# Keys in chunks of 128 with one chunk shared by two heads, in a fused attention and MLP kernel

## The chip, the cores and the metric

The kernel runs on one core of a Trainium2 chip. The metric is the device time of one execution in microseconds (us), taken from several executions; all times here are of executions in the undisturbed ("fast") state. Lower is better. Besides its times, each kernel left one profiled execution: a page of summaries and a trace of every instruction. The span of a profiled execution is a little off the median time (460.4 us profiled against 461.6 us for the kernel before).

## The reference

Attention over 8 batches of 12 heads, 448 tokens, 64 columns a head, with normalised queries and keys; then an MLP on the joined heads. Everything is float32 on the outside.

```python
def rmsnorm(x, g):
    return x / np.sqrt(np.mean(x * x, axis=-1, keepdims=True) + 1e-06) * g

q_n, k_n = rmsnorm(q, g_q), rmsnorm(k, g_k)              # (8, 12, 448, 64)
attn = softmax(q_n @ k_n.T / 8)                          # (cut: written out in the original)
x = (attn @ v).transpose(0, 2, 1, 3).reshape(3584, 768)
h = x @ w_in                                             # w_in (768, 2048)
g = h * (1.0 / (1.0 + np.exp(-1.702 * h)))
out = g @ w_out                                          # w_out (2048, 768)
```

## The kernel before

Heads are taken two at a time: 6 pairs in a batch, 48 in all. A pair goes through this line of stages. The sync queue loads queries, keys and values. ScalarE squares, VectorE sums, GpSimd finishes the norm and multiplies queries and keys into `row` (bf16). For the first 12 pairs TensorE turns `row` into columns; for the other 36 the sync queue does, with a transposing DMA. TensorE then makes the scores, ScalarE the exponential, TensorE the values, VectorE the division, and the sync queue turns the result into `xT` with another transposing DMA. The MLP matmuls `gp` (448 columns) and `op` (384 columns) of earlier batches are woven between. The output rows are stored by the sync queue too.

```python
SS, NS = 112, 4                    # 448 keys = 4 chunks of 112, for each head
N_ATT, N_KZ, N_V, N_RAW, N_SQ, N_QKN = 3, 3, 4, 7, 2, 3   # raw: loads of 7 pairs ahead

def load(i, which):                # one DMA for queries, one for keys, one for values
    src = (q, k, v)[which][b, h0:h0 + 2].rearrange("h (ss ns) d -> ss h ns d", ns=NS)
    ...
    eng = nc.scalar if i == 0 and which == 1 else nc.sync
    eng.dma_start(out=raw[i][:SS, which], in_=src)

def score(i, kc):                  # two matmuls a tile, four tiles a pair: 8 of 448 columns
    sc = scs[i, kc] = ps_sc.tile([128, 2, 512], FP32, tag="sc", name="sc")
    for hp in range(2):
        nc.tensor.matmul(sc[:SS, hp, :S], lhsT=qk_ring[i % N_KZ][:, NS * (1 + hp) + kc, :],
                         rhs=qk_ring[i % N_KZ][:, :NS, :], start=True, stop=True)

def values(i, hp, qs):             # 4 key chunks x 4 query chunks x 2 heads: 32 of 65 columns
    for kc in range(NS):
        nc.tensor.matmul(os_[i, hp][:, qs, :],
                         lhsT=att_ring[i % N_ATT][:SS, kc, hp, qs * SS:qs * SS + WIN],
                         rhs=vx_ring[i % N_V][:SS, hp, kc, :],
                         start=(kc == 0), stop=(kc == NS - 1))
```

The instruction order is not written by hand. A small list scheduler in the kernel simulates all engines with a duration for each task and writes the instructions in the order that it finds; the order on every engine and queue is then fixed. A task's arguments are the engine, the duration in ns, a priority and what it depends on.

```python
od.add(("L", i, w), "SP", 400, lambda i=i, w=w: load(i, w), i - 7 + (0, 0.1, 1.5)[w],
       deps=..., lat=moved(830.0))
od.add(("T", i), "SP", 400, lambda i=i: turn_dma(i), i - 10.0, deps=..., lat=moved(2400.0))
od.add(("X", i), "SP", 400, lambda i=i: back_dma(i), i - 10, deps=..., lat=moved(800.0))
od.add("gG", "DVE", 350, scale_g, -90, at=5000.0)      # product of the two gain vectors
for c in range(4):                                     # weights, by the GpSimd queue
    od.add(("WI", c), "POOL", 900, ..., at=13000.0 + 6500.0 * c, lat=moved(4100.0))
```

Of the kernel before, what the change touches and what calls it, by code (L numbers as in the profile page):

```python
# [9 lines left out]
FP32 = mybir.dt.float32  # L10
# [114 lines left out]

@with_exitstack
def kernel(
# [15 lines left out]
    assert DM == H * D  # L143
    SS = 112
    NS = S // SS
    NP = H // 2
# [24 lines left out]
    for t, src in ((gq, g_q), (gk, g_k)):  # L171
        col = src.rearrange("(d o) -> d o", o=1)
        for lo in (0, 64):
            nc.gpsimd.dma_start(out=t[lo:lo + 64, :], in_=col)  # L174
# [4 lines left out]
    att_ring = [consts.tile([128, NS, 2, AW], BF16, name=f"att{j}", tag=f"att{j}")  # L179
                for j in range(N_ATT)]  # L180

    qk_ring = [consts.tile([128, 3 * NS, SS], BF16, name=f"qk{j}", tag=f"qk{j}")
               for j in range(N_KZ)]


    row_ring = [consts.tile([128, (3 * NS + 1) * 128], BF16, name=f"row{j}", tag=f"row{j}")
                for j in range(N_QKN)]

    def row_view(j, gi):
        t = row_ring[j % N_QKN]  # L190
        if gi == 0 or j < ON_PE:
            t = t[:, gi * NS * 128:(gi + 1) * NS * 128]
            return t.rearrange("p (n h d) -> p h n d", h=2, d=D)
        both = t[:, NS * 128:].rearrange("p (h r) -> p h r", h=2)[:, :, :NS * 128]
        return both.rearrange("p h (n c) -> p h n c", c=128)[:, :, :, :D]

    vx_ring = [consts.tile([128, 2, NS, D + 1], BF16, name=f"vx{j}", tag=f"vx{j}")
               for j in range(N_V)]
    for t in qk_ring:
        nc.vector.memset(t[64:128, NS:2 * NS, :], 0.0)  # L200
        nc.vector.memset(t[0:64, 2 * NS:, :], 0.0)
    for t in vx_ring:
        nc.gpsimd.memset(t[:, :, :, D:D + 1], 1.0)
    for t in att_ring:
        nc.gpsimd.memset(t[:, :, :, S:AW], 0.0)
# [5 lines left out]
    raw_p = pool("raw", N_RAW)  # L211
    vraw_p = pool("vraw", N_RAW)
# [25 lines left out]
    raw, vraw, rs, obs, xT = {}, {}, {}, {}, {}  # L238
# [5 lines left out]
    def load(i, which):  # L244
        b, h0 = i // NP, 2 * (i % NP)
        src = (q, k, v)[which][b, h0:h0 + 2].rearrange("h (ss ns) d -> ss h ns d", ns=NS)
        if which == 2:
            vraw[i] = vraw_p.tile([128, 2, NS, D], FP32, tag="vraw", name="vraw")
            nc.sync.dma_start(out=vraw[i][:SS], in_=src)
            return  # L250
        if which == 0:
            raw[i] = raw_p.tile([128, 2, 2, NS, D], FP32, tag="raw", name="raw")
        eng = nc.scalar if i == 0 and which == 1 else nc.sync
        eng.dma_start(out=raw[i][:SS, which], in_=src)  # L254

    def square(i, part):
        if part.start in (None, 0):
            sq_of[i] = sq_p.tile([128, 2, 2, NS, D], FP32, tag="sq", name="sq")
        nc.scalar.activation(out=sq_of[i][:SS, part], in_=raw[i][:SS, part], func=ACT.Square)  # L259

    def reduce(i, part):
        g0 = group_of[i][0]
        if g0 not in ssq_of:
            ssq_of[g0] = stat_p.tile([128, 3, 2, 2, NS], FP32, tag="ssq", name="ssq")
        nc.vector.reduce_sum(out=ssq_of[g0][:SS, i - g0, part], in_=sq_of[i][:SS, part],  # L265
                             axis=AX.X)


    def stat_of(grp, name):
        t = stat_p.tile([128, 3, 2, 2, NS], FP32, tag=name, name=name)  # L270
        return t, t[:SS].rearrange("p a b c d -> p (a b c d)")[:, :len(grp) * 4 * NS]
# [3 lines left out]
    def seed(grp):  # L275
        x = ssq_of[grp[0]][:SS].rearrange("p a b c d -> p (a b c d)")[:, :len(grp) * 4 * NS]
        _, t = stat_of(grp, "seed")
# [6 lines left out]
    def rsqrt(grp):  # L284
        eng = nc.vector if grp[0] == 0 else nc.gpsimd
        x, t = seed_of[grp[0]]
        y, yf = stat_of(grp, "rs")
        m = len(grp) * 4 * NS
        eng.tensor_tensor(out=yf.bitcast(I32), in0=magic[:SS, :m], in1=t.bitcast(I32),  # L289
# [7 lines left out]
        for p in grp:  # L297
            rs[p] = (y, p - grp[0])

    def norm(i, gi):  # L300
        y, a = rs[i]
        if gi == 1 and ON_PE <= i < ON_PE + N_QKN:
            c = row_ring[i % N_QKN][:, NS * 128:3 * NS * 128].rearrange("p (n c) -> p n c", c=128)
            nc.gpsimd.memset(c[:, :NS, D:], 0.0)
            nc.gpsimd.memset(c[:, NS:, :D], 0.0)
        nc.gpsimd.tensor_tensor(  # L306
            out=row_view(i, gi)[:SS], in0=raw[i][:SS, gi],
            in1=y[:SS, a, gi].to_broadcast([SS, 2, NS, D]), op=ALU.mult)

    def vcast(i):  # L310
        vx = vx_ring[i % N_V][:SS].rearrange("p h n d -> p (h n) d")
        vr = vraw[i][:SS].rearrange("p h n d -> p (h n) d")
        nc.gpsimd.tensor_tensor(out=vx[:, :, :D], in0=vr,  # L313
                                in1=ones[:SS, :].to_broadcast([SS, 2 * NS, D]), op=ALU.mult)
# [12 lines left out]
    def take_q(i):  # L327
        nc.vector.tensor_copy(out=qk_ring[i % N_KZ][:, :NS, :], in_=tps[i][:, 0])
# [281 lines left out]
```

## Time and profile before

| quantity | before |
|---|---|
| time, median of 3 (range) | 461.67 us (461.55 to 461.86) |
| profiled span | 460.4 us |
| TensorE / ScalarE / GpSimd busy | 95% / 70% / 43% of the span |
| TensorE share of the chain that ended last | 88% |
| squares' wait for key loads, all executions of that instruction together | 9.1 us |
| sync queue's records, 100 to 300 us | 66% of the time, 59% without semaphore instructions |

The busy shares and the chain stand on the page. The squares' wait is a line of the view of waits by releaser.

How to read it: TensorE is the limit when its pieces follow each other without a gap, and then the time is the sum of its issue intervals. The prediction shows the lines for that.

### The profile page before, as it was taken

The numbers are of one execution on the slowest core, as the hardware profiler recorded it, in microseconds if no ns is written. First come the engines' busy times: TensorE is split into PE (matmuls) and PEld (weight loads), VectorE is DVE, ScalarE is ACT, GpSimd is POOL, SyncE is SP. The second block draws the span as 40 slices with busy tenths as digits, with TensorE's granted clock in tenths as the row PEclk, the third lists the DMA queues.
The fourth block names the chain that finished last, engine by engine and source line by source line (L and its number), as shares of the span: only waits on it lengthen the run. The fifth ranks groups of instructions, "written<-read, shape, count | busy, mean of one in ns | idle before, by whom it ended". The sixth has DMA issues, their size and how long they took to land.

```text
span 460.4 us, 9576 instructions
## 1 busy us (share of the span) xinstructions
PE 435.3 (95%) x3728; PEld 271.9 (59%) x3728; DVE 219.0 (48%) x471; ACT 324.1 (70%) x463; POOL 196.5 (43%) x319
## 2 busy tenths in 40 slices
PE   0589999999999999999999999999999999999995
PEld 0356666666666665666666665666666665665563
DVE  3777888765653446515572347622551125403400
ACT  4587997888887778967886779866786677614421
POOL 4888986975272544434452635445343000000000
PEclk9997999999999999999999999999999999999998
DMA  8999999966868866587675885575323650021022
GB/s 204 266 243 255 250 244 231 214 185 158 163 136 155 234 160 152 130 186 166 155 168 119 216 192 131 124 172 144 66 57 74 105 121 16 17 78 36 0 70 69
DMA packets 111277, 67.48 MB, mean 147 GB/s; under 512 B 70272, under 2 KB 107648, under 8 KB 111232
## 3 DMA queue, kind: packets, MB, share of 16 engines
q1 hardware_dynamic: 105616, 60.35, 56.0%
q0 software_dynamic: 5376, 6.29, 7.8%
q8 instruction: 29, 0.48, 0.5%
q10 hardware_dynamic: 240, 0.23, 0.2%
q14 instruction: 16, 0.13, 0.1%
HBM read 45.61 MB, written 11.01 MB: 123 GB/s over the span
## 4 chain that ended last, share of the span: by engine, by line
PE 88%; POOL 3%; DVE 2%; DMA 2%; ACT 2%; issue 1%; SPq 1%; POOLq 0%; DVEq 0%; ACTq 0%
PE op L514 32%; PE gp L491 30%; PE sc L350 15%; PE o L362 10%; DMA gk<-in_g_k_dram 1%; POOL row L306 1%; ACT att L355 1%; PE t_ps L322 1%; DMA raw<-in_k_dram 1%; PE ot_ps L385 1%; DVE ssq L265 1%; DVE qk L332 0%; DVE obs L373 0%; POOL gq L174 0%; SPq L254 0%
## 5 line engine op out<-in xcount | busy, mean ns | idle before, releaser
L355 ACT ACTIVATE att<-sc 112x896 bf16<-112x896 f32 x192 | 173.9, 916 | 39.9 <-PE sc L350 37.9
L514 PE MATMUL op<-w_out_s,g 128*128 128x384 bf16 x896 | 167.5, 325 | 0.0
L491 PE MATMUL gp<-xt,w_in_s 128*128 128x448 bf16 x768 | 162.6, 352 | 0.0
L306 POOL TENSOR_TENSOR row<-raw,rs 112x512 bf16<-112x512 f32 x96 | 98.3, 1043 | 94.2 <-DMA qk<-row 84.6
L350 PE MATMUL sc<-qk 128*112 128x448 bf16 x384 | 109.4, 370 | 3.0 <-ACT att L355 1.4
L514 PEld LDWEIGHTS <-g 128*128 128x128 bf16 x896 | 81.1, 97 | 47.4 <-issue 0.3
L506 DVE SCALAR_TENSOR_TENSOR g<-th,gp 128x448 bf16<-128x448 f32 x128 | 78.0, 615 | 60.9 <-ACT th L500 60.8
L491 PEld LDWEIGHTS <-w_in_s 128*128 128x128 bf16 x768 | 71.0, 98 | 57.8
L362 PEld LDWEIGHTS <-att 112*128 112x128 bf16 x1536 | 82.2, 99 | 36.8 <-DVE obs L373 1.5
L500 ACT ACTIVATE th<-gp 128x448 f32<-128x448 f32 x128 | 69.3, 543 | 35.3 <-PE gp L491 35.1
L362 PE MATMUL o<-vx,att 112*128 112x65 bf16 x1536 | 90.8, 196 | 0.7 <-ACT att L355 0.4
L313 POOL TENSOR_TENSOR vx<-vraw,ones 112x512 bf16<-112x512 f32 x48 | 50.0, 1042 | 51.6 <-PE o L362 35.8
L265 DVE TENSOR_REDUCE ssq<-sq 112x16 f32<-112x1024 f32 (+1 forms) x50 | 58.4, 1174 | 27.9 <-ACT sq L259 27.7
L372 DVE RECIPROCAL rcp<-o 112x4 f32<-112x4 f32 x96 | 17.4, 181 | 112.0 <-PE o L362 111.4
L259 ACT ACTIVATE sq<-raw 112x1024 f32<-112x1024 f32 (+1 forms) x50 | 50.9, 1022 | 14.3 <-DMA raw<-in_k_dram 9.1
L524 ACT ACTIVATE osb<-op 128x384 f32<-128x384 f32 x56 | 27.3, 487 | 40.4 <-PE op L514 40.4
L350 PEld LDWEIGHTS <-qk 128*112 128x112 bf16 x384 | 44.0, 135 | 17.9 <-issue 4.0
L373 DVE TENSOR_TENSOR obs<-o,rcp 112x256 bf16<-112x256 f32 x96 | 40.7, 424 | 3.3
L343 ACT ACTIVATE qk<-qk,gG 128x448 bf16<-128x448 bf16 x36 | 23.9, 663 | 1.0 <-DMA qk<-row 0.9
L322 PE MATMUL t_ps<-ident,row 112*128 112x112 bf16 x96 | 9.6, 250 | 15.8 <-POOL row L306 15.7
L322 PEld LDWEIGHTS <-row 112*128 112x128 bf16 x96 | 7.2, 117 | 19.0 <-POOL row L306 17.5
L289 POOL TENSOR_TENSOR rs<-magic,seed 112x48 int32<-112x48 int32 (+1 forms) x16 | 4.5, 282 | 20.0 <-DVE seed L280 16.9
(37 smaller groups left out, 90.1 us busy)
## 6 DMA issues: line engine op xcount, KB each, us to landing
raw<-in_q_dram SPq DMA_DIRECT2D x48, 224.0 KB, 4.2
vraw<-in_v_dram SPq DMA_DIRECT2D x48, 224.0 KB, 3.9
raw<-in_k_dram SPq DMA_DIRECT2D x47, 224.0 KB, 4.7
w_in_s<-in_moe_w_in_dram POOLq DMA_DIRECT2D x4, 768.0 KB, 12.8
w_out_s<-in_moe_w_out_dram POOLq DMA_DIRECT2D x4, 768.0 KB, 11.3
out_dram<-osb SPq DMA_DIRECT2D x8, 336.0 KB, 3.3
out_dram<-osb SPq DMA_DIRECT2D x8, 288.0 KB, 2.7
out_dram<-osb SPq DMA_DIRECT2D x8, 240.0 KB, 2.9
```

The lines of the kernel that those rows point to most:

```text
L259: nc.scalar.activation(out=sq_of[i][:SS, part], in_=raw[i][:SS, part], func=ACT.Square)
L265: nc.vector.reduce_sum(out=ssq_of[g0][:SS, i - g0, part], in_=sq_of[i][:SS, part], axis=AX.X)
L306: nc.gpsimd.tensor_tensor(out=row_view(i, gi)[:SS], in0=raw[i][:SS, gi], in1=y[:SS, a, gi].to_broadcast([SS, 2, NS, D]), op=ALU.mult)
L313: nc.gpsimd.tensor_tensor(out=vx[:, :, :D], in0=vr, in1=ones[:SS, :].to_broadcast([SS, 2 * NS, D]), op=ALU.mult)
L350: nc.tensor.matmul(sc[:SS, hp, :S], lhsT=qk_ring[i % N_KZ][:, NS * (1 + hp) + kc, :], rhs=qk_ring[i % N_KZ][:, :NS, :], start=True, stop=True)
L355: nc.scalar.activation(out=att_ring[i % N_ATT][:SS, kc, :, :S], in_=scs.pop((i, kc))[:SS, :, :S], func=ACT.Exp)
L362: nc.tensor.matmul(os_[i, hp][:, qs, :], lhsT=att_ring[i % N_ATT][:SS, kc, hp, qs * SS:qs * SS + WIN], rhs=vx_ring[i % N_V][:SS, hp, kc, : ...
L373: nc.vector.tensor_tensor(out=obs[i][:SS, :, hp, :], in0=o[:SS, :, :D], in1=rcp[:SS, :].to_broadcast([SS, NS, D]), op=ALU.mult)
L491: nc.tensor.matmul(ps[:, :], lhsT=w_in_s[:, ki, m * 128:(m + 1) * 128], rhs=xT[b][:, ki, :], start=(ki == 0), stop=(ki == KI - 1))
L500: nc.scalar.activation(out=th[:, :], in_=gps[b, m][:, :], func=ACT.Tanh, scale=0.851)
L506: nc.vector.scalar_tensor_tensor(out=g_of[b // 2][:, m, lo:lo + S], in0=ths.pop((b, m))[:, :], scalar=1.0, in1=gps.pop((b, m))[:, :], op0= ...
L514: nc.tensor.matmul(ops[bp, tm, hf][:, :], lhsT=g_of[bp][:, ko, tm * 128:(tm + 1) * 128], rhs=w_out_s[:, ko, hf * HALF:(hf + 1) * HALF], st ...
```

## The change

448 is 3 x 128 + 64. From the third batch on, a head's keys are three chunks of 128 and a tail of 64, and the tails of both heads share one chunk. That is 7 score matmuls a pair where there were 8, and all of them use the whole width of the array. The values follow: one matmul of 130 columns serves both heads' tails, with zeros in the other head's place. The loads of keys and values become three DMAs: one for the 2 x 384 rows, and one for each head's tail, which has to land on its own half of the partitions. GpSimd's multiplies are cut along the same line. Partition rows that the narrow form leaves unwritten must be zero, hence seven memsets at the start, and the gain vectors move from GpSimd's queue to the sync queue.

```diff
+    NB = 3
+    NC = 2 * NB + 1
+    TAIL = NB * 128
...
-    for t, src in ((gq, g_q), (gk, g_k)):
-        col = src.rearrange("(d o) -> d o", o=1)
-        for lo in (0, 64):
-            nc.gpsimd.dma_start(out=t[lo:lo + 64, :], in_=col)
...
+    for t in raw_ring:
+        nc.gpsimd.memset(t[96:128, :QW], 0.0)
...
     def load(i, which):
...
+        if which == 0 or not wide(i):          # as before: one DMA
...
             return
+        nc.sync.dma_start(out=by_head(t, (NB + 1) * D, NB * D, lo),
+                          in_=src[:, :TAIL].rearrange("h (p j) d -> p h (j d)", j=NB))
+        for h in range(2):
+            nc.sync.dma_start(out=t[HALVES[h], lo + NB * D:lo + (NB + 1) * D],
+                              in_=src[h, TAIL:])
...
+        for c in chunks(i, t):                 # 7 chunks in 4 tiles
+            nc.tensor.matmul(sc[parts_of(i), c % 2, :S], lhsT=keys, rhs=queries(i),
+                             start=True, stop=True)
...
+        one(NB, o, vx[:, NB:NB + 2, :], start=True, stop=False)   # 130 columns
+        for h in range(2):
+            for j in range(NB):
+                one(c, o[:, h, :], vx[:, c + h, :], ...)          # 65 columns
...
-    od.add("gG", "DVE", 350, scale_g, -90, at=5000.0)
+    od.add("Lg", "SP", 1700, load_g, PLACE["G"], lat=3000.0)
+    od.add("gG", "DVE", 350, scale_g, PLACE["gG"], deps=["Lg"])
...
-            od.add(("L", i, w), "ACTQ" if i == 0 and w == 1 else "SP", 400,
+            od.add(("L", i, w), "ACTQ" if i == 0 and w == 1 else "SP",
+                   1200 if w_ and w else 400,
```

(Cut: the same tiles as rings with views for both widths, the divisions' new layout, durations of the order's model.)

## The prediction

> **What bounds the kernel now.** I read the page first (busy shares, the 40 slices, the chain that ended last), then the chain in order of time for a steady stretch, then the groups by shape, then the timeline of the first 20 us.
>
> ```profile
> PE 435.3 (95%) x3728; PEld 271.9 (59%) x3728; DVE 219.0 (48%) x471; ACT 324.1 (70%) x463; POOL 196.5 (43%) x319
> PE   0589999999999999999999999999999999999995
> PE 88%; POOL 3%; DVE 2%; DMA 2%; ACT 2%; issue 1%; SPq 1%; POOLq 0%; DVEq 0%; ACTq 0%
> ```
>
> TensorE is busy in every slice but the first few and the last, and 88% of the chain that ended last is TensorE following itself. Busy time alone is no proof (ends of matmuls are modelled), so I looked at how closely the pieces follow each other:
>
> ```profile
> 204.52 0.13 PE o L362 x4
> 204.65 0.40 PE sc L350 x2
> 205.05 1.30 PE op L514 x8
> ...
> 209.22 0.38 PE sc L350 x2
> 209.60 0.65 PE op L514 x4
> 210.25 0.26 PE o L362 x8
> ```
>
> Each piece starts where the last one ends; nobody is waited for. So from about 55 us to the end the time is the sum of TensorE's issue intervals, and any interval that goes comes off the end. From start to start in the records between 100 and 400 us, the means are: 189 ns a score or gp matmul (448 columns), 162.5 an op (384), 32.2 a value matmul (65 columns). One oddity: a score pair takes 0.38 us after an MLP matmul but 0.40 after a value matmul. In the records the first score after a value matmul takes 209 ns and not 189 (68 of 68 cases, of 284 scores in that stretch).
>
> ```profile
> L350 PEld LDWEIGHTS <-qk 128*112 128x112 bf16 x384 | 44.0, 135 | 17.9 <-issue 4.0
> L362 PEld LDWEIGHTS <-att 112*128 112x128 bf16 x1536 | 82.2, 99 | 36.8 <-DVE obs L373 1.5
> ```
>
> The weight load of a score, 112 columns wide, takes 135 ns; all loads of 128 columns take 97 to 99. Behind a 32 ns value matmul the longer load is not hidden.
>
> The start is another regime. TensorE's first matmul is at 13.7 us:
>
> ```profile
> 0.75 0.90 SPq L254 DMA_DIRECT2D raw<-in_q_dram  x2
> 9.62 0.56 DVE L397 TENSOR_TENSOR gG<-gq,gk 128x1 f32<-128x1 f32 x1 [3.00 <-DMA gk<-in_g_k_dram]
> 12.61 2.04 POOL L306 TENSOR_TENSOR row<-raw,rs 112x512 bf16<-112x512 f32 x2 [2.46 <-DVE rs L296]
> ```
>
> VectorE stands 3.00 us for the gain vectors, fetched by GpSimd's queue, though only the key scaling needs them; behind that wait stand the eleven small operations of the first pair's norms (10.28 to 12.53 us), and behind these the first norm multiply at 12.61.
>
> **What the Trainium skill says.** (1) "TensorE: Matmul & The Clock Gate", section "Back-to-back issue gap", gives N/2.4 + 2.5 ns warm: 189.2 for 448 columns, 162.5 for 384. The trace agrees to the tenth. For 65 columns it gives 29.6 where I measure 32.2, so something else adds 2.6 ns there. For the new 130-column matmul I use 56.7. (2) The same page, section "Weight-path perf modes — Fast Weight Load (FWL) and DoubleRow", says the fast load needs exactly 128 weight columns. The 135 against 99 ns above agrees. (3) "DMA: Bandwidth & Descriptors", section "Why small descriptors are slow (HBM only)": a fixed cost for each packet. In the trace's packet records the median is 18 ns for 256 bytes, 46 for 1024 and 121 for 3072, that is 9 ns plus 0.0365 a byte: the fixed part is there and small. (4) "GPSIMD Engine Reference", section "Reconciling with measured numbers": a dispatch cost for each instruction and some 2.6 cycles an element; the trace's 1043 ns for 512 columns against 286 for 48 gives 208 ns fixed plus 1.63 ns a column.
>
> **The change part by part.** The first 12 pairs (two batches) keep their form; 36 pairs change.
>
> Scores, on the path: 7 in place of 8 a pair. 36 x 189 ns = **6.8 us off**.
>
> Values, on the path: 32 matmuls of 65 columns become 24 of 65 and 4 of 130 (one holds both heads' 64 tail keys, other head's values zero). 32 x 32.2 = 1030 ns; 24 x 32.2 + 4 x 56.7 = 1000 ns. 36 x 0.03 = **1.1 us off**.
>
> Weight loads, on the path: the key chunks are now 128 columns wide, so the 209 ns should become about 192 (what gp takes after a value matmul in the records). 68 cases among 284 scores, thus about 69 in 288: 69 x 17 ns = **1.2 us off**.
>
> Sum for TensorE: 9.1 us. The built program has 3548 matmuls in place of 3728, with the same 768 gp and 896 op.
>
> The start, on the path: the gain vectors now come by the sync queue and VectorE's order has them after the first norms, so the 3.0 us wait is off the chain. Against it stand seven new memsets of 32 x 512 on GpSimd before all else, and in the built program each query load waits for its memset. I estimate 0.52 us for one: the trace's memsets took 204 ns for 128 columns and 310 for 256, so 0.83 ns a column. The first query load then issues near 2.0 instead of 0.75 us. It lands near 5.0 and not 4.6 because the queue is shorter behind the key load. Then sum of squares near 6.9, norm chain to 9.2, first norm multiply at 9.3 instead of 12.6. Further on the gain shrinks: the second pair's key load is later in the queue, VectorE waits for it, and the first scores I put at 14.2 instead of 16.6. Before the first MLP matmul the scalar engine's order has one more square (1.06 us) than before, with equal counts of exponentials. Net **1.7 us off** (2.4 less some of the 1.06).
>
> Beside the path: ScalarE evacuates a single chunk in the fourth score tile, 543 ns (the row of the tanh, same 448 columns) for 916: 36 x 0.37 = 13 us less. VectorE reduces 960 columns for 1024: about 2 us less. GpSimd pays: the key multiply and the value copy become four instructions each, 2 x (208 + 192 x 1.63) + 2 x (208 + 64 x 1.63) = 1.67 us for 1.04. That is 36 x 1.25 = 45 us more, some 245 us in all (54%), still far from a bound. DMA: a key or value load is 256 packets of 768 bytes plus 128 of 256 in place of 224 of 1024: 11.8 for 10.3 engine-us, little. It is three issues instead of one on the sync queue, 36 x 4 x 0.42 = 60 us more issue time, on a queue that loads pairs seven ahead.
>
> I add **0.6 us** for waits that do not exist now: 461.7 - 9.1 - 1.7 + 0.6 = **451.5**, rounded to 451.3 since the start may give its whole 2.4.
>
> **The rivals.** (a) The start gives nothing or loses: the memsets of GpSimd may run slower than 0.83 ns a column (f32 and not bf16), and the loads of pairs 0 to 2 queue behind four tiny transfers. For it speaks that everything before 20 us hangs on the loads; against it that the 3 us wait is plainly removed. Then 453 to 454. (b) The scalar engine becomes the wait: squares of later pairs already wait for key loads (9.1 us in ten cases in the waits by releaser, the longest 2.6), and these loads now land about 1 us later, being three issues; a scalar stall past some 2 us would hold the PSUM tiles and so TensorE. Against it: the scheduler's order in the built program was made with the longer loads, and ScalarE has 13 us more room. At its worst 36 x 0.1 = 4 us: 455. (c) The score's extra 20 ns is not the narrow load; then 1.2 us less gain: 452.5. (d) GpSimd falls behind between 60 and 100 us, where it is 74 to 80% busy in the windows and the first wide pairs, with their extra memsets, begin; the values would wait for their copies. Its later waits for the row transposes (84.6 us) say there is room: at most 2 us. (e) Upward: the start gives 4 us: 449.
>
> **Range and chances.** The TensorE sum is firm, 8 to 9.5 us: 452.2 to 453.7 by itself, all but at the 2% line of 452.4. The start decides the side. With my 1.7 it is faster; with (a) or (b) within 2%. Predicted 451.3, 449.0 to 454.3, faster 0.67, within 2% 0.32, slower 0.01 (no engine comes near a new bound).
>
> **What the profile after would show.** Right: TensorE still in nearly all of the chain; 252 wide scores at 189 ns, also behind value matmuls, with loads near 99 ns; the 130-column ones about 57 ns apart; first matmul between 10 and 12 us; first scores near 14. Wrong: idle time before score or op matmuls put down to ScalarE, VectorE's first reduce later than 5.3 us by over 2, squares waiting much more than 9 us in total for key loads, or the value matmuls of 65 columns no longer 32 ns.

## The result and the profile after

| | before | after |
|---|---|---|
| time, median (range), 4 runs each, same chip | 461.61 us (461.06 to 461.86) | 467.00 us (465.40 to 467.55) |
| ratio after / before (95% interval) | | 1.0113 (1.0084 to 1.0141) |
| profiled span | 460.4 us | 465.5 us |

The kernel became 1.1% slower, which is still within 2%. A ratio here is always the mean time of one kernel's fast runs over the mean of the other's of the same rounds, so it is not quite the ratio of the medians in the table. The prediction was 451.3 us with a range from 449.0 to 454.3; the result is well outside.

First the page of the changed kernel: busy time of each engine, the 40 slices of TensorE, and the chain that ended last, by engine and by line.

```profile
PE 427.3 (92%) x3548; PEld 259.0 (56%) x3548; DVE 215.3 (46%) x471; ACT 306.1 (66%) x463; POOL 233.7 (50%) x543
PE   0767899999999988999899998999999999999995
PE 66%; DMA 17%; issue 5%; SPq 4%; POOL 3%; ACT 2%; DVE 2%; ACTq 0%; POOLq 0%; DVEq 0%
```

TensorE has 180 matmuls less and is busy 8 us less, as hoped, but its slices now show 8s in the middle. The chain holds 66% TensorE where it held 88%. What came in its place is DMA with 17%, and the sync queue (SPq) with 4%.

How much time TensorE stood still is read from the view of windows. Its columns are the window, its length, then busy us (and instructions) of PE, PEld, DVE, ACT and POOL, then the granted clock (the share of TensorE's full clock that it was given), the DMA engines' share and GB/s. Before, then after:

```profile
140.00:180.00 40.00, 39.82 (x356) 25.24 (x355) 17.15 (x38) 31.05 (x45) 16.98 (x24) 1.00 0.77 171
180.00:220.00 40.00, 40.00 (x352) 25.35 (x350) 17.31 (x36) 31.00 (x45) 19.18 (x33) 1.00 0.73 167
```

```profile
140.00:180.00 40.00, 36.85 (x312) 22.47 (x311) 12.82 (x29) 24.51 (x39) 23.94 (x61) 1.00 0.77 172
180.00:220.00 40.00, 37.97 (x316) 22.88 (x314) 18.63 (x40) 31.39 (x48) 23.18 (x59) 1.00 0.66 158
```

TensorE stood for 3.15 and 2.03 us in these two windows, and hardly at all before. Over the whole stretch from 60 to 400 us the same view gives 339.46 us busy of 340 before and 329.98 after: 0.5 against **10.0 us idle**. In these two windows the granted clock is 1.00 on both sides, and the DMA engines' share is not higher than before.

What it waited for is read from the view of waits by releaser. Its columns are the total us, the number of times and the longest wait. Before, then after:

```profile
ACT sq L259 <- DMA raw<-in_k_dram: 9.1, 10, 2.6
ACT qk L343 <- DMA qk<-row: 0.9, 1, 0.9
```

```profile
ACT sq L300 <- DMA raw<-in_k_dram: 26.2, 19, 2.9
ACT qk L416 <- DMA qk<-row: 8.0, 7, 2.4
```

ScalarE's squares wait 26 us for key loads where they waited 9, and its scaling of the turned queries waits 8 us for the transposing DMA where it waited 1. ScalarE itself has less to do than before, but it stands in order, so these waits hold the exponentials behind them.

The next view is the chain in order of time (start us, us, what) around one of the stalls of the changed kernel. "SPq" is the sync queue issuing.

```profile
172.31 0.42 SPq L652
...
173.17 0.41 SPq L291
...
174.83 0.58 SPq L291
...
175.46 0.48 SPq L294
175.94 0.04 issue
175.98 4.13 DMA raw<-in_k_dram
...
180.22 1.01 ACT sq L300
...
182.53 0.42 DVE obs L469
182.95 0.54 DVE g L623
...
183.53 1.29 PE gp L608 x6
```

The key load, 4.13 us from the end of its issue to its landing, is the last link before the square. It is in the queue behind an output store (L652) and a value load (L291 and L294), and the chain goes through all of them: the queue worked them off one after another. After the square, VectorE's sum, division and gate follow, and the gate (g) is what the MLP matmul at 183.53 waits for.

The timeline of the sync queue shows the same stretch from its own side: start us, us, line, operation, tile, and xN where N DMAs are folded into one row. Before, then after:

```profile
171.47 1.90 SPq L338 DMA_TRANSPOSE qk<-row  x1
173.81 1.20 SPq L392 DMA_TRANSPOSE xt<-obs  x1
175.12 0.52 SPq L249 DMA_DIRECT2D vraw<-in_v_dram  x1
178.51 0.31 SPq L254 DMA_DIRECT2D raw<-in_q_dram  x1
```

```profile
169.95 1.69 SPq L412 DMA_TRANSPOSE qk<-row  x1
171.76 0.97 SPq L652 DMA_DIRECT2D out_dram<-osb  x2
173.17 0.41 SPq L291 DMA_DIRECT2D vraw<-in_v_dram  x1
173.64 1.14 SPq L294 DMA_DIRECT2D vraw<-in_v_dram  x2
174.83 0.58 SPq L291 DMA_DIRECT2D raw<-in_k_dram  x1
175.46 1.13 SPq L294 DMA_DIRECT2D raw<-in_k_dram  x2
176.68 1.23 SPq L490 DMA_TRANSPOSE xt<-obs  x1
```

Before, the queue has pauses: nearly 3 us between 175.64 and 178.51. After, one issue follows the other with hardly a gap. Counted over 100 to 300 us the queue's records fill 66% of the time before and **89%** after. Part of that is semaphore instructions, which issue nothing; the DMA issues alone fill 59% before and **87%** after. With the mean lengths of its records in that stretch this can be added up for one pair, in us:

| for one pair | before | after |
|---|---|---|
| transposing DMA of queries and keys | 1.57 | 1.59 |
| transposing DMA of the result | 1.30 | 1.30 |
| query load | 0.46 | 0.61 |
| key load | 0.53 | 0.50 + 2 x 0.51 |
| value load | 0.68 | 0.71 + 2 x 0.57 |
| output stores | 0.44 | 0.56 |
| sum | 4.98 | 7.43 |

24 pairs pass in these 200 us, so a pair has 8.3 us. 4.98 of 8.3 is 0.60 and 7.43 of 8.3 is 0.89; the direct counts are 0.59 and 0.87, since not quite every DMA of 24 pairs falls into the stretch. The semaphore instructions are the rest: 0.07 before, most of it ahead of the transposing DMAs, and 0.02 after.

What the change was made for did come. The groups by shape, in the changed kernel (busy us and mean ns after the bar):

```profile
L430 PEld LDWEIGHTS <-qk 128*128 128x128 bf16 x252 | 22.9, 98 | 15.8
L454 PE MATMUL o<-vx,att 128*128 128x130 bf16 x144 | 31.8, 221 | 3.4 <-DVE obs L469 3.4
```

The wide score's weight load takes 98 ns where the narrow one took 135, and there are 252 of them, 7 for each of the 36 pairs. From start to start, a score behind a value matmul now takes 188.6 ns and not 209. The 130-column matmul takes 57 to 58 ns from start to start.

### The profile page after: what moved, and what is told of

Same layout as the page of the kernel before. It is cut to its first block, busy times and chain, and to the rows that moved or that the text cites. A ratio compares the mean times of both kernels' runs of the same rounds, so it can differ in the third digit from the quotient of the medians.

```text
span 465.5 us, 9795 instructions
## 1 busy us (share of the span) xinstructions
PE 427.3 (92%) x3548; PEld 259.0 (56%) x3548; DVE 215.3 (46%) x471; ACT 306.1 (66%) x463; POOL 233.7 (50%) x543
## 4 chain that ended last, share of the span: by engine, by line
PE 66%; DMA 17%; issue 5%; SPq 4%; POOL 3%; ACT 2%; DVE 2%; ACTq 0%; POOLq 0%; DVEq 0%
PE op L631 26%; PE gp L608 24%; DMA raw<-in_k_dram 9%; PE sc L430 9%; DMA vraw<-in_v_dram 8%; PE o L454 6%; POOL row L349 2%; SPq L288 1%; ACT sq L300 1%; SPq L294 1%; PE o L446 1%; DVE g L623 1%; POOL vx L349 1%; SPq L291 1%; ACT att L435 1%
## 5 line engine op out<-in xcount | busy, mean ns | idle before, releaser
L435 ACT ACTIVATE att<-sc 128x896 bf16<-128x896 f32 (+1 forms) x192 | 159.7, 846 | 32.0 <-PE sc L430 31.3
L349 POOL TENSOR_TENSOR row<-raw,rs 64x64 bf16<-64x64 f32 (+3 forms) x204 | 115.4, 588 | 83.1 <-DMA qk<-row 55.4
L430 PE MATMUL sc<-qk 128*128 128x448 bf16 (+1 forms) x348 | 100.5, 366 | 6.3 <-ACT att L435 4.2
L313 DVE TENSOR_REDUCE ssq<-sq 128x15 f32<-128x960 f32 (+2 forms) x50 | 56.2, 1127 | 60.4 <-ACT sq L300 56.8
L349 POOL TENSOR_TENSOR vx<-vraw,ones 128x192 bf16<-128x192 f32 (+2 forms) x156 | 66.7, 446 | 29.6 <-PE o L454 13.3
L300 ACT ACTIVATE sq<-raw 128x960 f32<-128x960 f32 (+2 forms) x50 | 48.9, 983 | 34.4 <-DMA raw<-in_k_dram 26.2
L454 PEld LDWEIGHTS <-att 128*128 128x128 bf16 x1008 | 53.0, 98 | 28.4 <-DVE obs L469 4.7
L454 PE MATMUL o<-vx,att 128*128 128x65 bf16 (+1 forms) x1008 | 57.8, 198 | 5.4 <-DVE obs L469 3.4
L641 ACT ACTIVATE osb<-op 128x384 f32<-128x384 f32 x56 | 27.3, 487 | 40.5 <-PE op L631 40.4
L446 PEld LDWEIGHTS <-att 112*128 112x128 bf16 x384 | 18.9, 103 | 9.0 <-ACT att L435 1.9
L446 PE MATMUL o<-vx,att 112*128 112x65 bf16 x384 | 21.4, 201 | 1.8 <-ACT att L435 1.3
L397 PE MATMUL t_ps<-ident,row 112*128 112x112 bf16 x96 | 9.8, 255 | 13.9 <-POOL row L349 13.7
```

What stands on the lines that cost most here:

```text
L300: nc.scalar.activation(out=sq_of[i][parts_of(i), part], in_=raw_ring[i % N_RAW][parts_of(i), part], func=ACT.Square)
L313: nc.vector.reduce_sum(out=stats(i, ssq_of[g0])[:, part.start // D:part.stop // D], in_=sq_of[i][parts_of(i), part].rearrange("p (c d) -> ...
L349: nc.gpsimd.tensor_tensor(out=out, in0=in0, in1=by, op=ALU.mult)
L430: nc.tensor.matmul(sc[parts_of(i), c % 2, :S], lhsT=keys, rhs=queries(i), start=True, stop=True)
L435: nc.scalar.activation(out=att_of(i)[parts_of(i), c.start:c.stop, :S], in_=scs.pop((i, t))[parts_of(i), :len(c), :S], func=ACT.Exp)
L446: nc.tensor.matmul(o[:, w, :], lhsT=att[:SS, 2 * kc + u, w * SS:w * SS + WIN], rhs=vx[:SS, u * NS + kc, :], start=(kc == 0), stop=(kc == N ...
```

## The experiments

Fourteen kernels ran. All gave correct results. A kernel is compared with runs of the kernel before on the same chip. The table gathers what is used below: median time, ratio to the kernel before with its 95% interval, TensorE's idle time between 60 and 400 us (340 less the busy time in the view of windows), and the share of the time between 100 and 300 us that the sync queue's records fill, first all records, then DMA issues alone. (The expectations speak of the first of these.) The last three are from the profiled execution.

| kernel | us | ratio (95%) | idle us | sync records / issues |
|---|---|---|---|---|
| before | 461.6 | 1 | 0.5 | 0.66 / 0.59 |
| after | 467.0 | 1.0113 (1.0084 to 1.0141) | 10.0 | 0.89 / 0.87 |
| 1 before, loads in three | 466.17 | 1.0099 (1.0072 to 1.0127) | 4.2 | 0.85 / 0.81 |
| 2 before, small packets | 465.54 | 1.0082 (1.0064 to 1.0100) | 2.0 | 0.68 / 0.62 |
| 3 before, start of after | 465.32 | 1.0076 (1.0054 to 1.0099) | 0.7 | 0.64 / 0.58 |
| 4 after, one tail DMA | 455.47 | 0.9860 (0.9833 to 0.9887) | 1.0 | 0.74 / 0.73 |
| 5 after, start of before | 464.55 | 1.0075 (1.0047 to 1.0104) | 7.6 | 0.90 / 0.89 |
| 6 before, gain product late | 463.66 | 1.0041 (0.9992 to 1.0091) | 0.0 | 0.63 / 0.58 |
| 7 = 4 + 5 | 455.77 | 0.9854 (0.9807 to 0.9901) | 0.9 | 0.74 / 0.72 |
| 8 = 4, memsets late | 456.17 | 0.9879 (0.9841 to 0.9917) | 0.8 | 0.72 / 0.71 |
| 9 = 4, weights late | 460.75 | 0.9959 (0.9901 to 1.0016) | 6.9 | 0.73 / 0.71 |
| 10 = 7, weights late | 452.93 | 0.9810 (0.9781 to 0.9840) | 0.3 | 0.74 / 0.72 |
| 11 before, weights late | 468.22 | 1.0145 (1.0123 to 1.0166) | 2.9 | 0.61 / 0.58 |
| 12 = 6, weights late | 464.19 | 1.0053 (1.0023 to 1.0083) | 1.2 | 0.63 / 0.58 |
| 13 after, stores elsewhere | 462.18 | 1.0004 (0.9982 to 1.0027) | 6.2 | 0.85 / 0.84 |
| 14 = 10, stores elsewhere | 457.22 | 0.9878 (0.9838 to 0.9918) | 4.8 | 0.70 / 0.68 |

The theory after the first comparison was that the middle of the kernel is lost to the sync queue's issue time, and that the start loses by its own. The rivals were the smaller packets of the tails (256 bytes), GpSimd's longer copies, and the start alone.

How single a change is can be read from the traces, by comparing the order of the instructions on each engine with that of the kernel which was edited. In experiments 1, 2 and 4 every engine runs the same instructions in the same order, but for the number of load issues on the sync queue; in 8 (compared with 4) only the seven memsets stand elsewhere. In all the others the scheduler found another order on every engine: in 3 and 6, for instance, some 740 of TensorE's 3728 matmuls stand elsewhere. Those runs show what a version costs, but not cleanly what the one edit costs.

### 1. The kernel before with its loads cut in three

Nothing else of the change is in this kernel: same widths, same packets.

```diff
+    def send(eng, t, src, i):
+        cuts = (0, SS) if i < ON_PE else (0, 48, 80, SS)
+        for lo, hi in zip(cuts, cuts[1:]):
+            eng.dma_start(out=t[lo:hi], in_=src[lo:hi])
...
-            nc.sync.dma_start(out=vraw[i][:SS], in_=src)
+            send(nc.sync, vraw[i], src, i)
...
-        eng.dma_start(out=raw[i][:SS, which], in_=src)
+        send(eng, raw[i][:, which], src, i if which else 0)
```

> The kernel before, but from pair 12 on each key and value load is cut into three DMAs by partitions (48, 32, 32); packets stay 1024 bytes, no other instruction moves on any engine. Theory A (the sync queue's issue time is the new limit): its share between 100 and 300 us rises from 0.65 to about 0.9 as in the changed kernel, squares wait over 20 us for key loads instead of 9, and the time rises by 5 to 10 us, to 467-471. Rival B (smaller packets or the transposes of 128 rows delay the loads) and rival C (GpSimd's longer norms and copies): nothing of theirs is in this kernel, so 461.7 within 1 us.

It took 466.17 us, 4.5 us more than the kernel before. The queue's share rose to 0.85, the squares' wait for key loads to 17.6 us in 16 cases, and TensorE idled 4.2 us. Each of these is just under what was expected. So more issues alone do cost time here; they do not make the whole 10 us at this share.

### 2. The kernel before with small packets

```diff
+        src = (q, k, v)[which][b, h0:h0 + 2]
+        src = src.rearrange("h (ns ss) d -> ss h ns d", ns=NS) if which and i >= ON_PE else \
+            src.rearrange("h (ss ns) d -> ss h ns d", ns=NS)
```

One DMA a load as before, but every key and value packet is 256 bytes and not 1024, which is worse than in the changed kernel.

> The kernel before, but from pair 12 on keys and values are fetched in runs of 256 bytes (896 packets a load instead of 224), still one DMA for a load; keys are permuted alike in both, so the result stays right. Theory A (issue time): a load is still one issue, so the time stays within 1.5 us of 461.7 unless the issue itself takes longer with more packets (then by as much as the queue's share shows). Rival B (DMA packets): this more than doubles the packet time of a load (16 engine-us for 10), over what the change added, so the loss must be at least that of the change in mid-kernel, 8 to 10 us.

It took 465.54 us, 3.9 us more than the kernel before: over the 1.5 us that theory A allowed, and under the 8 that rival B asked for. Where, the view of windows shows:

```profile
60.00:100.00 40.00, 38.08 (x336) 23.91 (x335) 29.58 (x59) 31.06 (x43) 28.35 (x53) 0.96 1.10 216
100.00:140.00 40.00, 40.00 (x356) 25.02 (x355) 22.94 (x48) 33.99 (x50) 23.07 (x42) 1.00 0.73 157
```

There is a stall of 1.9 us before 100 us, soon after the first small-packet loads, and next to nothing after it, at a queue share of 0.68. The clock of 0.96 there is, by the trace's clock records, a stretch of 3.4 us, from 82.3 us, at half the clock, in which a matmul of 448 columns took 373 ns and not 189; that is worth some 1.7 us (an estimate, half of the stretch). So small packets came with a loss before 100 us, but they do not make the stalls of the middle. The same run shows that the issue time goes with the number of DMAs far more than with their packets: a key load of four times as many packets took 0.53 us to issue, as before, and a value load 0.75 for 0.68.

### 3. The kernel before with the start of the changed kernel

The seven memsets, the gains by the sync queue and the late product, without any wide chunk.

```diff
-            nc.gpsimd.dma_start(out=t[lo:lo + 64, :], in_=col)
+    for t in raw_ring:
+        nc.gpsimd.memset(t[96:128, 0], 0.0)
...
-    od.add("gG", "DVE", 350, scale_g, -90, at=5000.0)
+    od.add("Lg", "SP", 1700, load_g, -5.2, lat=3000.0)
+    od.add("gG", "DVE", 350, scale_g, -0.5, deps=["Lg"])
```

> The kernel before with only the start of the changed one: seven memsets of the raw tiles ahead of all else on GpSimd, the gain vectors by the sync queue after the first four loads, VectorE's product of them after the first norms. Theory D (the start costs): first score near 15.0 us as in the changed kernel, but loads of pairs 7 to 9 land 4 to 6 us later than before, squares wait for them, and TensorE has 3 to 4 us less work done by 60 us: time 464.5 to 466. Rival E (the start is harmless, TensorE's deficit at 60 us in the changed kernel comes from the wide loads that begin at 42 us): 459.5 to 461.7.

It took 465.32 us. The start of the changed kernel, with the order that the scheduler then finds, costs 3.7 us; the prediction had it as a gain of 1.7. Hardly any of it is idle time after 60 us, so it is lost before that.

### 4. The changed kernel with two DMAs a load

The tails of two neighbouring heads can be read in one DMA if the heads are cut the other way: the first head gives its first 384 keys to the wide chunks and its last 64 to the shared chunk, the second head its last 384 and its first 64. The two tails then lie next to each other in memory as 128 rows. The order of keys does not matter to attention. Everything else stays: widths, GpSimd's copies, the start.

```diff
         nc.sync.dma_start(out=by_head(t, (NB + 1) * D, NB * D, lo),
-                          in_=src[:, :TAIL].rearrange("h (p j) d -> p h (j d)", j=NB))
-        for h in range(2):
-            nc.sync.dma_start(out=t[HALVES[h], lo + NB * D:lo + (NB + 1) * D],
-                              in_=src[h, TAIL:])
+                          in_=bass.AP(tensor=src.tensor, offset=src.offset,
+                                      ap=[[NB * D, 128], [(TAIL + 128) * D, 2], [1, NB * D]]))
+        nc.sync.dma_start(out=t[:, lo + NB * D:lo + (NB + 1) * D],
+                          in_=src.rearrange("h s d -> (h s) d")[TAIL:TAIL + 128])
```

> The changed kernel with two DMAs instead of three for each wide key and value load: both heads' tails are taken as the 128 rows that lie together in memory (the last 64 of one head, the first 64 of the next), same bytes and packets, no other instruction moves. Theory A: two issues of some 0.55 us less a pair of about 9 us, the sync queue's share falls from 0.90 to about 0.78, squares wait some 12 us instead of 26, and the time falls by 4 to 7 us, to 460-463. Rivals B and C: packets and GpSimd work are the same, so 466 to 467.

It took **455.47 us**: 11.5 us less than the changed kernel and 1.4% faster than the kernel before. Theory A had expected 4 to 7 us, so it had the direction and not the size. Its windows:

```profile
140.00:180.00 40.00, 40.00 (x337) 24.28 (x334) 18.02 (x38) 31.15 (x50) 24.98 (x64) 1.00 0.86 182
180.00:220.00 40.00, 39.68 (x333) 24.01 (x332) 18.61 (x40) 29.02 (x45) 21.11 (x55) 1.00 0.75 173
```

```profile
ACT sq L300 <- DMA raw<-in_k_dram: 12.0, 9, 2.5
```

TensorE is full again, and the squares' wait is back near its old 9.1 us. Tail packets are as small and GpSimd's copies as long as in the changed kernel, and every engine runs the same instructions in the same order but for the one issue less in each load, so neither is the cause.

### 13. The changed kernel with its stores on another queue

Experiment 4 changes the loads themselves, so it could be that three transfers are late in themselves and the queue has no part in it. This one leaves every load as it is and takes other work off the queue.

```diff
-            nc.sync.dma_start(
+            nc.scalar.dma_start(
                 out=out[b * S:(b + 1) * S].rearrange(...)
...
-            od.add(("D", bp, tm), "SP", 1200, ...
+            od.add(("D", bp, tm), "ACT", 1000, ...
```

> The changed kernel with nothing different but the queue of its output stores: they are issued by the scalar engine's queue, which evacuates the rows that they store. No load, packet, tile or matmul differs. Theory Q (issue time on the sync queue): some 60 stores of 0.48 us, 29 us, leave the sync queue, so its busy share between 100 and 300 us falls from 0.90 to about 0.83; by the two points on hand (0.85 share cost 4.5 us in the first experiment, 0.76 next to nothing) the stall of 10 us between 140 and 320 us should shrink to 3 to 5, the squares' wait for key loads from 26 to about 17, and the time fall by 4 to 7 us, to 460 to 463; the scalar engine has 27 us more to do and may give 1 us back. Rival T (a load in three transfers is late in itself, whatever else the queue does, since three completions must come in): the stall stays, 466 to 468. Rival G (the GpSimd engine's longer copies hold the chain): the same, 466 to 468.

It took 462.18 us, 4.8 us less than the changed kernel, inside what the queue theory gave and outside what the two rivals gave. The share fell to 0.85, a little less than expected, and the squares' wait to 19.8 us. The idle time between 140 and 320 us fell from 9.5 to 5.2 us, where 3 to 5 had been expected. That is not far from experiment 1, which came to nearly the same share from the other side, by adding issues to the kernel before. But the scheduler gave every engine another order here, so this run alone does not isolate the queue.

Rival T can be settled in the traces. From the start of its first issue to its last landing, a key load between 100 and 300 us took 3.46 us (median) in three DMAs in the changed kernel, 3.68 in two in experiment 4, and 3.89 in one in the kernel before. Three transfers are not late in themselves; they are issued late. With experiments 1 and 4, in which only the number of issues differs, this shows the cause in the middle: it is the issue time on this queue.

### 5 to 8. The start

Experiment 5 takes the start of the change back in the changed kernel: gains by GpSimd's queue, memsets by VectorE just before the first wide pairs use the tiles.

```diff
-    for t in raw_ring:
-        nc.gpsimd.memset(t[96:128, :QW], 0.0)
+        if which == 0 and ON_PE <= i < ON_PE + N_RAW:
+            nc.vector.memset(t[96:128, :QW], 0.0)
...
-    od.add("Lg", "SP", 1700, load_g, PLACE["G"], lat=3000.0)
-    od.add("gG", "DVE", 350, scale_g, PLACE["gG"], deps=["Lg"])
+    od.add("gG", "DVE", 350, scale_g, PLACE["gG"], at=9500.0)
```

> The changed kernel, still three issues a wide load, but with the start of before: gain vectors by GpSimd's queue at once, no memsets ahead of the loads (each raw tile's bottom rows are cleared by VectorE just before its first wide use); VectorE's product of the gains stays behind the first norms. Theory D (the start of the changed kernel costs 3 to 4 us): 462.5 to 464.5, with the mid-kernel losses of 10 us still there. Rival E (its start deficit comes from the wide loads at 42 us or from scatter): 466 to 468.

It took 464.55 us, 2.4 us less than the changed kernel's median (467.00, of another chip's rounds); the two intervals overlap, so a gain is not sure. In its trace 25.3 us of matmul work had begun by 60 us (24.1 in the changed kernel, counted with the steady issue intervals), and the idle time after 60 us is 2.4 us less, so at most a part of the difference lies in the start.

Experiment 6 makes the one edit in the kernel before that the prediction counted on: VectorE multiplies the gains after the first norms. (The scheduler's order changes with it.)

```diff
-    od.add("gG", "DVE", 350, scale_g, -90, at=5000.0)
+    od.add("gG", "DVE", 350, scale_g, -0.5, at=9500.0)
```

> The kernel before with one move: VectorE's product of the gains behind the first pairs' norms, so the 3.0 us wait is gone; loads as before. The prediction's step (that wait is on the path, worth about 2 us at the end): 459.3 to 460.3, first score near 14.3 us. Rival F (the start is limited by the loads, which land 0.86 us apart, and by the weight loads that share the DMA engines, so an earlier first score is given back): 461 to 463, with the same lost TensorE time by 60 us, 32 us.

The first scores came at 14.0 us and not 16.6, as the prediction says, and yet the time was 463.66 us, with an interval that holds "no change" and leaves out a gain of more than 0.1%. A wait was taken away on the chain to the first score, and the end did not come earlier. The first MLP matmul started at 57.9 us, where the kernel before has it at 55.0. A rival that no run separates is TensorE's clock: before 60 us it stood at half for 13.7 us in this trace and for 6.8 us in the kernel before, and the fastest of the four runs (459.82 us) had a mean clock of 0.993, the other three (463.47 to 465.79 us) 0.983 to 0.987.

Experiments 7 (4 and 5 together) and 8 (4 with late memsets, but the gains by the sync queue) ask whether start and middle add up.

> One tail issue (as in the fourth run) and the start of before with the late gain product. If mid-kernel issue time and the start are the two causes and add: 455.5 less about 3, 451.5 to 453.5; with lost TensorE time (span less the sum of issue intervals) 38 to 40 us as in the kernel before. If the start's cost was already only scatter in the fourth run (33.1 us lost by 60 us, 32.1 before): 454.5 to 455.5.

> The fourth run's kernel with the memsets taken from ahead of the loads, the gain vectors still by the sync queue: splits the start's cost. If the four gain transfers on the sync queue (2.6 us of issue before the third pair's loads) are the cost: 455 to 456. If the memsets (the first query load at 1.94 instead of 0.75 us) are: 453 to 454, near the run with both mended.

They took 455.77 and 456.17 us, no better than experiment 4. With two DMAs a load, taking the start back is worth nothing that these runs can see. Experiment 8 is the cleanest of these, since nothing but the memsets moved: its first score came at 13.7 us, where experiment 4 has it at 15.7, and the time did not fall. Here too the clock stood at half for longer before 60 us, 17.1 us against 6.8.

### 9 to 12. The weights later

The four loads of `w_in` run beside the key loads of pairs 7 to 9. In the changed kernel these key loads land at 30.8, 36.6 and 40.5 us, and at 25.1, 30.5 and 35.5 before. The theory was that an earlier weight load takes their bandwidth. Each experiment issues `w_in` later in the order's model: 9 in kernel 4, 10 in kernel 7, 11 in the kernel before, 12 in kernel 6.

```diff
-    WI=13000.0, WIs=6500.0, WO=42000.0, WOs=7000.0)
+    WI=19000.0, WIs=6500.0, WO=42000.0, WOs=7000.0)
```

> The fourth run's kernel (one tail issue, start as changed) with the four issues of the first weight matrix some 5 us later in GpSimd's order; they landed at 30 to 49 us and the first MLP matmul comes at 56. Theory W (an earlier start only lets the weights share the DMA engines before the loads of pairs 7 to 9 are in, so their squares wait): those key loads land by 26, 30 and 35 us instead of 31, 37 and 41, TensorE has lost 31 to 32 us by 60 us instead of 33 to 36, and the time falls from 455.5 to 451.5-453.5. If the weights don't matter: 455 to 456.

> The seventh run's kernel (one tail issue, start of before, gain product late) with the weights some 5 us later: theory W 450 to 452.5, because the first score is 1 to 2 us sooner than in the kernel before and is kept; if the weights don't matter: 455 to 456.

> The kernel before with the weights some 5 us later alone, as control. Before, the loads of pairs 7 and 8 already landed 3 to 5 us ahead of their squares, only pair 9 waited 1.14 us, so theory W gives little: 459.5 to 461.5. If it gains over 3 us, the weights' place was a fault of the kernel before and not something the change brought about.

> The sixth run's kernel (the kernel before, gain product late, first score at 14.0 us instead of 16.6, yet 463.7 us) with the weights some 5 us later. Theory W: the early start is now kept, 458.5 to 460, TensorE's lost time by 60 us 29 to 31 us instead of 34.7. If the cause is another (slower loads from the start on, or TensorE's clock falling to half): 462.5 to 464.

The key loads came earlier in all four (pair 9 at 28 to 33 us), as foreseen. The times did not follow. Experiment 10 is the best kernel with **452.93 us**, 1.9% faster than the kernel before. Experiment 9 lost 5 us against kernel 4, experiment 11 lost 6.5 us against the kernel before, and experiment 12 changed nothing (464.19 against 463.66), which its expectation had kept for another cause. In experiment 9 the loss has moved:

```profile
60.00:100.00 40.00, 33.69 (x284) 21.04 (x282) 25.82 (x55) 26.84 (x39) 25.76 (x57) 0.91 0.86 196
```

TensorE stands for 6.3 us there, and the clock of 0.91 is two stretches of 3.4 us at half (from 65.2 and 78.8 us), worth another 3.4 us (an estimate, half of both). Two squares wait 4.1 and 2.5 us for key loads, and the chain in order of time has a value load of 15.0 us and a key load of 11.2 us that end in this stretch, later loads than those that were freed. So the theory holds for the landing times and fails for the total. What brought the new waits about was not isolated, since the order changed on every engine too.

The page of experiment 10, slices and chain:

```profile
PE   0678799999999999999999999999999999999995
PE 86%; DVE 6%; DMA 3%; POOL 2%; issue 1%; ACT 1%; SPq 0%; POOLq 0%; ACTq 0%
```

TensorE is back in 86% of the chain, and every slice from the sixth to the last but one is full.

### 14. Experiment 10 with its stores on the scalar queue

> The best version so far (both tails in one transfer, gains by the GpSimd queue, memsets late, weights late) with its stores on the scalar engine's queue as well. Theory Q: its sync queue is at about 0.76 and no stall is left between 100 and 400 us, so the 29 us of issue time that go are worth nothing: 452 to 454, or 1 us more for the scalar engine's 27 us. If it gains more than 2 us, the queue still cost something in the start, before 100 us.

It was to be the control of 13: where the queue has room, moving the stores should give nothing. It took 457.22 us, 4.3 us more than experiment 10, and so more than the 1 us that was allowed for. Its idle time is 2.1 us between 60 and 100 us and 2.7 us between 140 and 220 us, at a sync share of 0.70. So moving the stores has a price of its own: the order of the whole kernel changes, and ScalarE has to issue them. Which of the two it is was not tried, and its trace has 3.4 us at half the clock, from 74.2 us, that experiment 10 does not have. So the 4.8 us of experiment 13 are a net figure of a queue with room, more work on ScalarE and another order.

## Why the prediction was wrong

**TensorE's sum: right.** 36 scores of 189 ns are gone: 6.8 us. The values of a pair went from about 1040 to 1000 ns from start to start, 1.4 us in all. The 68 scores behind a value matmul lost their extra 20 ns, 1.4 us. That makes 9.6 us where the prediction has 9.1. Rival (c), that the 20 ns is not the narrow load, is ruled out by the 188.6 ns.

**New waits, put at 0.6 us: this step failed, and it is the larger error.** The prediction wrote down the new issue time on the sync queue, 60 us, and set it aside with "on a queue that loads pairs seven ahead". It never summed what the queue did already. The sum for the kernel before, 4.98 us a pair out of 8.3, could be had from its trace; with the added issues it is 7.43. The added term was too small as well: 7.43 - 4.98 is 2.45 us a pair, 88 us for 36 pairs. A ring of seven pairs helps against late landings only as long as the queue can issue the loads early, and in a queue that works in order, issues 87% of the time and also waits for the data of its transposing DMAs, it cannot. The trace shows how small the lead was already in the kernel before: from pair 24 on (counted from 0), the issue of a key load ended 2.8 to 6.9 us before its square began, less than the 8.3 us of one pair. In the changed kernel it was 1.4 to 4.3 us. Between 60 and 400 us TensorE idled 10.0 us, where the kernel before has 0.5. One of the prediction's own signs of being wrong came with it: squares that wait much more than 9 us for key loads.

**Rival (b) had the mechanism and not the size.** It named the squares' wait for key loads and the three issues, put the landing about 1 us later, and gave the whole at worst 4 us. The wait grew from 9.1 to 26.2 us, and the idle time by 9.5 us. Its reason against, that the order was made with the longer loads, also fell: the order's model charges 1200 ns for a wide load and 400 ns for a transposing DMA, and the trace has 1.5 to 1.9 us and 1.3 to 1.6 us. The model believed in a queue with room.

The Trainium skill has the rule that was needed: "Perfetto Trace Analysis", section "What "DMA-bound" means", lists the issuing engine's sequencer as a bound of its own, seen when its track is solid DMA slices. The trace agrees in kind; but DMA issues that fill 0.81 to 0.87 of the time (experiment 1 and the changed kernel), not solid, came with 4 to 10 us of idle time here.

**The start, put at -1.7 us: wrong in sign.** In the kernel before it cost 3.7 us (experiment 3, order changed with it). Single steps of it can be checked against the timeline of the changed kernel:

```profile
1.39 3.31 POOL L233 MEMSET raw<- 32x512 f32 x7
1.94 0.89 SPq L288 DMA_DIRECT2D raw<-in_q_dram  x2
5.26 1.28 ACT L300 ACT_TABLE_LOAD   x1 [5.26 <-DMA raw<-in_q_dram]
6.55 2.19 ACT L300 ACTIVATE sq<-raw 112x512 f32<-112x512 f32 x4
10.93 2.09 POOL L349 TENSOR_TENSOR row<-raw,rs 112x512 bf16<-112x512 f32 x2 [2.19 <-DVE rs L344]
```

The memsets come every 0.47 us (estimate 0.52), and the first query load is issued near 2.0 us as said. But ScalarE's table load, which ran at 1.2 us in the kernel before, beside the load, now stands behind the wait for it, so the first square starts at 6.55 us and not at 4.68. The first norm multiply comes at 10.9 us (predicted 9.3, before 12.6), and the first score at 15.0 (predicted 14.2, before 16.6). The wait for the gains is gone, as the prediction says. Rival (a) had the right side (the start loses), at less than half the size: it allowed 453 to 454 us, 1.7 to 2.7 us above the predicted time, where experiment 3 has the start 5.4 us above its term (3.7 for -1.7). What failed is the step from there to the end: that the first score's gain comes off the time. It did not in experiment 6, with a first score 2.6 us earlier, nor in experiment 8, 1.9 us earlier. Why the start loses stays open: the loads of the first ten pairs, the weights, the order and the clock before 60 us (at half for 6.8 us in the kernel before and 10.2 us in the changed one) were not separated.

**Together.** The profiled spans differ by +5.1 us: -9.6 for TensorE's sum, +9.5 for the idle time between 60 and 400 us, and a rest of +5.2. Of this rest 3.8 us lie before 60 us: counted with its steady issue intervals, the matmul work that TensorE had begun by then is 27.9 us in the kernel before and 24.1 in the changed one. The remaining 1.4 us, in small gaps, I have not placed. The prediction had -9.1, +0.6 and -1.7.

**The other terms.** GpSimd is busy 233.7 us (said: 245), ScalarE 18 us less (said: 13); both stayed beside the path, and rival (d) is ruled out by experiment 4, which has the same GpSimd work and hardly any idle time (1.0 us).

## What to carry to other kernels

Before cutting a load into pieces, add up what its queue already issues in one period of the steady state, with the lengths from the trace, and compare the sum with the period: a queue has a capacity like an engine. In the two pairs of kernels here that differ in the number of issues alone, TensorE idled 0.5 us where DMA issues filled 59% of the time and 4.2 us at 81% (before and experiment 1), and 1.0 us at 73% and 10.0 us at 87% (experiment 4 and after). The remedy that worked is fewer DMAs, by choosing which rows go together, as in experiment 4, which turned a loss of 1.1% into a gain of 1.4%. And what the removal of a wait in the start of a kernel is worth is not known until it is seen what the first long stretch of work then waits for.

## What the Trainium skill lacked or had wrong

- "DMA: Bandwidth & Descriptors", section "Issuing engines are not separate DMA queues", says that the issue time is usually small relative to the DMA itself. For one plain DMA that holds: 0.4 to 0.8 us to issue on average, against 3.0 us from issue to landing for the large part of a key load of the changed kernel. What is lacking is that the issues add up on one queue (87% of the time here), that a transposing DMA took 1.3 to 1.6 us to issue, and any figure for an issue.
- "Perfetto Trace Analysis", section "What "DMA-bound" means", says that large descriptors are what matters for a full issuing queue too. Here four times as many packets left the issue of a key load at 0.53 us (experiment 2), while two DMAs in place of three took the issues from 0.87 to 0.73 of the time and the time down by 11.5 us (experiment 4). (The same page's section "DMA Optimizations" does name batching small transfers into larger ones, and balancing DMAs across the engines that can issue them; experiment 13 did the second, and took 4.8 us less.)
- "TensorE: Matmul & The Clock Gate", section "Back-to-back issue gap": the prediction took its formula as it stands, but the section calls it the gap of an isolated matmul and says that in a stream of weight loads and matmuls it under-counts for few columns (81 ns measured for 128) and over-counts for many (131 ns for 512). Here, in such a stream, it agrees to about 1 ns for 448, 384 and 130 columns (189, 162 and 57 to 58 ns). Only for 65 columns does it under-count: it gives 29.6 ns, and the trace has 32 to 33 ns from one such matmul to the next, and 29.2 ns where a 130-column one came just before.
